# Block-sparse attention and a gated projection on one core: eleven more matmuls of ones by ones in the first three steps

## The chip, the core and the metric

The kernel runs on one core of one Trainium2 chip. A core has five engines that run their own instruction streams and wait for one another by semaphores: TensorE (PE in the rows; its weight loads are PEld), VectorE (DVE), ScalarE (ACT), GpSimd (POOL) and SyncE (SP), which here only issues transfers. TensorE reads SBUF and writes PSUM. The metric is the device time of one execution in microseconds; the median of the runs of the kernel before is 371.38 us.

## The reference, cut to what matters

Four batches, 8 heads, 768 positions in 24 blocks of 32, head size 64. The mask lets a block of queries see its neighbours, the first and the last block and three drawn blocks; the first and last blocks see everything.

```python
scores = scale * np.matmul(q, k.transpose(0, 1, 3, 2))
scores = np.where(mask, scores, -1000000000.0)
scores = scores - np.max(scores, axis=-1, keepdims=True)
attn = np.exp(scores)
attn = attn / (np.sum(attn, axis=-1, keepdims=True) + 1e-09)
out = np.matmul(attn, v)
# then, with x = the heads side by side (B, S, 512):
gate = 1.0 / (1.0 + np.exp(-gate_pre))   # gate_pre: a causal convolution of 5 taps over x
val = x @ w_val
result = gate * val @ w_out
```

## The kernel before, in words

The work is cut into units. A unit is a pair of neighbouring query blocks of one batch (11 pairs in a batch), or one of the two end blocks, for all 8 heads. The loop at line 762 runs over steps n, one unit entering per step. In a step the program issues, in this order for TensorE: the scores of unit n (`scores`, lines 409 to 466: 16 small f32 matmuls, which the trace shows as 32 passes, into two PSUM tiles `sc`, one for each half h of the heads), the product with the values of unit n-2 (`values`, line 479: `av<-va` and `av<-vb`), the transposition of a finished pair (`xp`), and the transposes of the weights of unit n-1 (`transposes`, line 468: `pt`), with matmuls of the projection (`vp`, `op`) put between them later on. Every engine executes its instructions in the order of the program; the class `InOrder` (line 77) ties each to the one before.

Between TensorE's pieces lie the other engines' parts: VectorE takes the row maxima of the scores (`mx`, line 457), ScalarE makes the exponentials from them (`pe`, line 462, two activations for each half h) and copies the transposes out of PSUM (`ptr`, line 475). GpSimd and ScalarE copy the key blocks of a pair together (`kg`, lines 326 to 348), ScalarE scales the queries (`qc`), and GpSimd gathers the value rows (`vb`).

The score tiles come from a pool of three buffers (line 71), two for each unit. So the second tile of unit 1 takes the buffer that the first half of unit 0 had, and the second tile of unit 2 the one that the first half of unit 1 had. Each must wait until ScalarE has read that half. Since the matmuls of the two halves alternate, everything behind them on TensorE waits with them.

At the very start there is nothing to multiply until queries and keys have arrived. There the program multiplies a tile of ones by itself 17 times into a PSUM tile `idle` that nothing reads (lines 110 to 114):

```python
    idle = ps_moe.tile([128, 512], F32, tag="mo", name="idle")
    for _ in range(WARM):
        matmul(idle[:, 0:256], ones[:, 0:128], ones, start=True, stop=True)
```

`idle` is one of two buffers of the tag "mo", which the transposition `xp` takes first in step 3.

Of the kernel before, what the change touches and what calls it, by code (L numbers as in the profile page):

```python
# [36 lines left out]
COPY_AHEAD = 2  # L37
WIDE, SPLIT = 2, 4
WARM = 17
HI_MOE = 2  # L40

COPIED = [{0: POOL, 1: POOL, 2: POOL, 3: ACT, 4: ACT, 5: ACT}, {0: POOL, 1: POOL, 2: ACT}, {}, {}]
# [22 lines left out]
def attention_moe(ctx, tc, qb, kb, v, ve, sampled, w_val, conv_w, w_out, ident_in, slot_in, out):  # L65
# [30 lines left out]
    matmul, transpose = pe.matmul, pe.transpose  # L96
# [13 lines left out]
    ones = const.tile([128, 256], F32, name="ones")  # L110
    pool.memset(ones, 1.0)
    idle = ps_moe.tile([128, 512], F32, tag="mo", name="idle")
    for _ in range(WARM):
        matmul(idle[:, 0:256], ones[:, 0:128], ones, start=True, stop=True)
    warm = const.tile([128, 1], F32, name="warm")
    dve.memset(warm, 0.0)
    act.activation(warm, warm, AF.Exp)
# [45 lines left out]
    def indices(b):  # L163

        row = const.tile([128, NB], F32, tag=f"row{b % 2}", name="row")
        dve.tensor_scalar_add(row, base, float(b * S - B * S))
        dve.tensor_tensor(out=row, in0=row, in1=valid, op=ALU.mult)
        dve.tensor_scalar_add(idx[:, b, :], row, float(B * S))
# [18 lines left out]
    def run(calls):  # L187
        while calls:
            calls.pop(0)()
# [106 lines left out]
    def block_numbers(pr, eng):  # L296

        mine = [n for n in range(2 * NR) if COPIED[pr.bt.b].get(n, SP) == eng]
        if not mine:
            return  # L300
        first = NR * PAIRS[pr.p][0] + mine[0]
        _, regs = nc.values_load_multi_w_load_instructions(
            sm[0:1, first : first + len(mine)], engines=[eng], min_val=0, max_val=NB - 1,
            skip_runtime_bounds_check_because="block numbers are drawn from [0, 24)",
        )
        for n, reg in zip(mine, regs):
            yield 5 + 4 * (n // NR) + n % NR, reg
# [101 lines left out]
    def scores(un):  # L409
        pr = un.pr  # L410
        un.P = []
        if pr.glob:
            lo = [ps_sc.tile([128, 512], F32, tag="sc", name="s0") for _ in range(2)]
            places = ((ps_moe, "mo"),) * 2 if pr.bt.b < HI_MOE else ((ps_sc, "sc"), (ps_pt, "pt"))
            hi = [space.tile([128, 512], F32, tag=tag, name="s1") for space, tag in places]
# [52 lines left out]
    def transposes(un):  # L468
        un.PT = []
        for p in un.P:  # L470
            pt = ps_pt.tile([128, 4, 128], F32, tag="pt", name="pt")
            for c in range(4):
                transpose(pt[:, c, :], p[:, 128 * c : 128 * c + 128], ident)
            t = three.tile([128, 4, 128], F32, tag="ptr", name="ptr")
            act.copy(t, pt)
            un.PT += [t[:, c, :] for c in range(4)]
            yield
# [43 lines left out]
    def finish(pr):  # L521
        if pr.p == 0:
            if pr.bt.b >= 2:

                while len(batches[pr.bt.b - 2].read) < 2 * len(TILES[pr.bt.b - 2]):
                    fill()
                    prepare(4)
            pr.bt.xT = two.tile([128, CH, KW - 1 + S], F32, tag="xT", name="xT")
            dve.memset(pr.bt.xT[:, :, 0 : KW - 1], 0.0)
        xT = pr.bt.xT  # L530
        near = units[max(step[0] - 1, 0) : step[0] + 1]
        spare = pr.bt.b < 2 and not may_project() and not any(un.pr.glob for un in near)
        space, tag = (ps_moe, "mo") if spare else (ps_sc, "sc")
        xp = space.tile([128, 4, 128], F32, tag=tag, name="xp")
        for j in range(2):
            transpose(xp[:, j, :], pr.x[:, j].rearrange("p h d -> p (h d)"), ident)
        yield
        o = KW - 1
        xv = xp[:, 0:2, :].rearrange("p j (c s) -> p c j s", c=CH)
        if pr.glob:  # L540
            for e, s0 in ((0, 0), (1, S - BLK)):
                act.copy(xT[:, :, o + s0 : o + s0 + BLK], xv[:, :, e, :])
        else:
            s0 = o + PAIRS[pr.p][0] * BLK
            act.copy(xT[:, :, s0 : s0 + 2 * BLK], xp[:, 0:2, :].rearrange("p a (b s) -> p (a b) s", b=2))
        pr.bt.done.add(pr.p)
        for t, (r0, rn) in enumerate(TILES[pr.bt.b]):
            need = {p for p in range(NP - 1) if any(r0 <= i * BLK < r0 + rn for i in PAIRS[p])}
            if r0 == 0 or r0 + rn == S:
                need.add(-1)  # L550
            if t not in pr.bt.queued and need <= pr.bt.done:
                pr.bt.queued.add(t)
                queue_rows(pr.bt, t)
# [128 lines left out]
    def store():  # L682
        while stores:
            sp.dma_start(*stores.pop(0))
# [27 lines left out]
    def may_project():  # L712
        return "all" in decoded and to_project and step[0] > max(to_project[0][0].ready)

    def fill(times=1):
        for _ in range(times):
            if may_project():
                run(late)
                advance(to_project)
# [21 lines left out]
    def freed(k):  # L741

        return units[min(k, N - 1)].pr.seq if k >= 0 else -1

    def more(which, upto, load):
        if at[which] < len(pairs) and pairs[at[which]].seq <= upto:
            load(pairs[at[which]])
            at[which] += 1
            return True

    def until(which, n, do):
        while at[which] < min(len(pairs), pairs.index(units[min(n, N - 1)].pr) + 1):
            do(pairs[at[which]])
            at[which] += 1
# [7 lines left out]
    for n in range(N + LAG_V):  # L762
        step[0] = n

        def more_keys():
            return more("keys", freed(n - 1) + RING, load_keys)

        def more_values():
            return more("values", freed(n - LAG_V - 1) + VRING, load_values)

        if n == 0:
            more_keys()
            numbers_first = {eng: list(block_numbers(pairs[0], eng)) for eng in (POOL, ACT)}
            until("scaled", 0, scale)
            indices(0)
            until("copied", 0, copy_keys)
            more_keys()
            until("copied", 1, copy_keys)
            more_values()
        else:  # L780
            while more_keys() or more_values():
                more_values()
        until("scaled", n + (SCALE_AHEAD if n else 1), scale)
        store()
        k = len(staged)
        if k < 2 * CH and n >= WEIGHTS_AT[k] and (k < 4 or k - 4 in decoded):
            next(weights)

        second_half = []
        if n < N:  # L790
            second_half.append(scores(units[n]))
            if not (n and units[n - LAG_T].pr.glob and units[n - LAG_T].pr.bt.b < HI_MOE):
                run(second_half)
        if n == 0:
            more_keys()
        until("copied", n + COPY_AHEAD, copy_keys)
        if n == 0:
            while more_keys() or more_values():
                more_values()
        if 0 <= n - LAG_V < N:  # L800
            values(units[n - LAG_V])
        if n >= LAG_V:
            while more("values", freed(n - LAG_V) + VRING, load_values):
                pass
        ending = [finish(units[n - LAG_X].pr)] if n >= LAG_X and units[n - LAG_X].last else []
        full = n < N and units[n].pr.glob and units[n].pr.bt.b >= HI_MOE
        for end in ending:
            if not full:
                next(end)

        def end_pairs():
            while ending:
                for _ in ending.pop(0):
                    pass

        if 0 <= n - LAG_T < N:
            pieces = 3 if units[n - LAG_T].pr.glob else 2
            for half, _ in enumerate(transposes(units[n - LAG_T])):
                at_half = 2 * n + min(half, 1)
                run(second_half)  # L820
                run(waiting)
                if half + 1 == pieces:
                    run(copies)
                    end_pairs()
                fill(int(FILLS[at_half]))
                holding[0] = half + 1 < pieces and not may_project()
                prepare(int(STEPS[at_half]))
                holding[0] = False
        else:
            fill(1)  # L830
            prepare(int(STEPS[2 * n]))
        if n == N + LAG_V - 1:
            ending.append(finish(units[N - 1].pr))
        end_pairs()
# [53 lines left out]
```

## Time and profile before

| what | value |
|---|---|
| three runs | 369.98, 371.38 and 376.13 us, median 371.38 us |
| the profiled execution | span 372.1 us; no other time of it is given |
| mean granted TensorE clock in it | 0.986 |
| busy: TensorE, VectorE, ScalarE, GpSimd | 94%, 73%, 68%, 39% of the span |
| TensorE in the chain that ended last | 78% of the span |

In a row of the timeline the first number is the start in us from the start of the span, the second the time from there to the end of the last instruction of the row. Instructions that follow one another and are alike share a row. The bracket tells how long the engine had been idle and what is thought to have ended that. The ends of matmuls are modelled, while a semaphore that another engine waits for is real: when VectorE starts a reduction, the scores are there. An f32 matmul has two passes, so a row of 34 passes stands for 17 matmuls. The rows of stretches give, for each stretch, its length, each engine's busy time, then the granted TensorE clock as a share of full speed, the share of the DMA engines and GB/s.

### The profile page before, as it was taken

Reading aid. Unit: us, or ns where it says so; the run is one execution under the profiler, and the core shown is the slowest. Engines: PE = TensorE matmul, PEld = TensorE weight load, DVE = VectorE, ACT = ScalarE, POOL = GpSimd, SP = SyncE. Lnnn points to the kernel's source line nnn. Section 1 sums busy time; section 2 is a strip of 40 time slices with the busy share of each in tenths; the row PEclk is TensorE's granted clock in tenths of the full one; section 3 lists DMA queues with packets and bytes.
Section 4 is the critical chain, followed back from the end, with each engine's and each line's share of the span. In section 5 each row is a group of like instructions: output and inputs, shape, how many; then the busy total and the mean of one; then the engine's idle time right before and its main releaser. Section 6 shows DMA issues by size and latency. Waiting matters only on the chain.

```text
span 372.1 us, 15481 instructions
## 1 busy us (share of the span) xinstructions
PE 349.9 (94%) x6274; PEld 276.1 (74%) x6274; DVE 270.6 (73%) x618; ACT 254.3 (68%) x619; POOL 144.9 (39%) x237
## 2 busy tenths in 40 slices
PE   8689998888998999999999999999999999999995
PEld 7456665556666787788779877787888779889894
DVE  4246789888978888678978867577669865979540
ACT  2568689899787857758687587666658766764421
POOL 1856683866573333633352063522531143000000
PEclk9959999999999999999999999999999999999999
DMA  7978886889987365798879367898664373110102
GB/s 229 278 241 277 283 281 226 237 219 299 286 257 248 109 167 146 188 315 232 262 203 289 107 173 214 218 288 250 192 195 130 98 232 99 55 58 28 75 11 85
DMA packets 52582, 72.35 MB, mean 194 GB/s; under 512 B 6944, under 2 KB 34720, under 8 KB 52512
## 3 DMA queue, kind: packets, MB, share of 16 engines
q1 hardware_dynamic: 44896, 47.69, 42.0%
q0 software_dynamic: 7040, 23.43, 22.1%
q8 instruction: 50, 0.82, 0.9%
q10 hardware_dynamic: 576, 0.24, 0.2%
q14 instruction: 20, 0.16, 0.2%
HBM read 65.05 MB, written 6.29 MB: 192 GB/s over the span
## 4 chain that ended last, share of the span: by engine, by line
PE 78%; DVE 8%; ACT 7%; issue 4%; another core or an unknown queue 1%; DMA 1%; ACTq 0%; DVEq 0%
PE vp L83 18%; PE op L83 18%; PE av L83 15%; PE pt L83 11%; PE sc L83 10%; PE xp L83 4%; PE s L83 3%; DVE mx L83 2%; ACT pe L83 2%; ACT ptr L83 2%; DMA sb<-in_sampled 1%; DVE xl L83 1%; DVE wst L83 1%; ACT first L83 1%
## 5 line engine op out<-in xcount | busy, mean ns | idle before, releaser
L83 POOL DMA_INDIRECT vb<-in_v,idx x88 | 87.4, 993 | 158.9 <-PE av L83 129.9
L83 ACT ACTIVATE pe<-sc,mx 128x256 f32<-128x256 f32 x176 | 69.6, 476 | 50.2 <-DVE mx L83 46.3
L83 DVE SCALAR_TENSOR_TENSOR th<-xT,cw,th 128x384 f32<-128x384 f32 x128 | 79.2, 626 | 7.5 <-ACT th L83 5.5
L83 DVE TENSOR_REDUCE mx<-sc 128x2 f32<-128x512 f32 x88 | 56.8, 684 | 38.1 <-PE sc L83 24.6
L83 ACT COPY ptr<-pt 128x512 f32<-128x512 f32 x112 | 64.4, 603 | 9.6 <-PE pt L83 7.1
L83 PE MATMUL sc<-kg,qc 64*32 64x256 f32 x1408 | 54.6, 388 | 6.9 <-DVE cst L83 3.4
L83 POOL COPY kg<-k 128x256 f32<-128x256 f32 (+1 forms) x143 | 56.8, 434 | 9.1 <-DMA k<-in_k 8.0
L83 PE MATMUL op<-wo,yh 128*128 128x512 f32 x192 | 53.6, 401 | 0.0
L83 PE MATMUL vp<-xh,wv 128*128 128x384 f32 x256 | 51.3, 341 | 0.0
L83 PE MATMUL pt<-ident,pe 128*128 128x128 f32 x352 | 50.9, 280 | 0.0
L83 PEld LDWEIGHTS av<-va,ptr 128*32 128x32 f32 (+1 forms) x1056 | 32.2, 119 | 24.9 <-issue 16.4
L83 PE MATMUL av<-va,ptr 128*32 128x65 f32 (+1 forms) x1056 | 42.7, 228 | 4.0 <-issue 3.1
L83 PEld LDWEIGHTS pt<-ident,pe 128*128 128x128 f32 x352 | 42.0, 144 | 3.3 <-DMA qc<-in_q 0.4
L83 PEld LDWEIGHTS vp<-xh,wv 128*128 128x128 f32 x256 | 44.2, 188 | 0.2
L83 PEld LDWEIGHTS sc<-kg,qc 64*32 64x32 f32 x1408 | 24.1, 107 | 26.9 <-issue 16.9
L83 PEld LDWEIGHTS op<-wo,yh 128*128 128x128 f32 x192 | 34.7, 188 | 6.6
L83 PE MATMUL av<-vb,ptr 128*32 128x65 f32 x1408 | 38.3, 224 | 1.3 <-issue 1.3
L83 PEld LDWEIGHTS av<-vb,ptr 128*32 128x32 f32 x1408 | 30.3, 111 | 3.3 <-issue 1.8
L83 PE MATMUL op<-wo,yl 128*128 128x512 f32 x96 | 31.6, 410 | 0.0
L83 ACT CAST yh<-y 128x384 fp32r<-128x384 f32 x32 | 16.6, 519 | 20.4 <-DVE y L83 19.8
L83 DVE SCALAR_TENSOR_TENSOR y<-th,vp 128x384 f32<-128x384 f32 x32 | 17.6, 549 | 13.7 <-PE vp L83 12.3
L83 PE MATMUL vp<-xl,wv 128*128 128x384 f32 x128 | 27.3, 335 | 0.0
(72 smaller groups left out, 441.1 us busy)
## 6 DMA issues: line engine op xcount, KB each, us to landing
kg<-in_k SPq DMA_DIRECT2D x165, 64.0 KB
vn<-in_v SPq DMA_DIRECT2D x12, 520.0 KB
qc<-in_q SPq DMA_DIRECT2D x48, 128.0 KB
k<-in_k SPq DMA_DIRECT2D x12, 512.0 KB
out<-ot SPq DMA_DIRECT2D x23, 256.0 KB
va<-in_v SPq DMA_DIRECT2D x44, 130.0 KB
wst<-in_w_val SPq DMA_DIRECT2D x4, 512.0 KB
wst<-in_w_out SPq DMA_DIRECT2D x4, 512.0 KB
```

Of the source, the lines that this page charges most:

```text
L83: made = getattr(self.eng, name)(*args, **kwargs)
```

## The change

The loop of the 17 matmuls becomes a function, and the steps n = 1 and n = 2 call it ahead of their scores, for 7 and for 4 more of the same matmul. They read and write what the first 17 did.

```diff
 WARM = 17
+MORE = {1: 7, 2: 4}
 HI_MOE = 2
...
-    for _ in range(WARM):
-        matmul(idle[:, 0:256], ones[:, 0:128], ones, start=True, stop=True)
+
+    def keep_busy(times):
+        for _ in range(times):
+            matmul(idle[:, 0:256], ones[:, 0:128], ones, start=True, stop=True)
+
+    keep_busy(WARM)
...
             next(weights)
 
+        keep_busy(MORE.get(n, 0))
         second_half = []
         if n < N:
             second_half.append(scores(units[n]))
```

On TensorE the first three steps read so before (kg_143 is the keys' buffer of unit 0, kg_144 of unit 1, kg_145 of unit 2; `pt` here are the transposes of unit 0):

```order
L83 MATMUL idle<-ones 128x256 x16
L83 MATMUL sc<-kg_143,qc 32x256 [waits Activation_49,Pool_49]
L83 MATMUL sc<-kg_143,qc 32x256 x15
L83 MATMUL sc<-kg_144,qc 32x256 [waits Activation_49,Pool_49]
L83 MATMUL sc<-kg_144,qc 32x256 [waits DVE_49,Activation_49]
L83 MATMUL sc<-kg_144,qc 32x256 x14
L83 MATMUL pt<-ident,pe 128x128 [waits DMAHW3_49]
L83 MATMUL sc<-kg_145,qc 32x256 [waits DVE_49,Activation_49,Pool_49]
L83 MATMUL sc<-kg_145,qc 32x256 [waits DVE_49,Activation_49]
L83 MATMUL sc<-kg_145,qc 32x256 x14
```

And so with the change:

```order
L84 MATMUL idle<-ones 128x256 x16
L84 MATMUL sc<-kg_143,qc 32x256 [waits Activation_49,Pool_49]
L84 MATMUL sc<-kg_143,qc 32x256 x15
L84 MATMUL idle<-ones 128x256 x7
L84 MATMUL sc<-kg_144,qc 32x256 [waits Activation_49,Pool_49]
L84 MATMUL sc<-kg_144,qc 32x256 [waits DVE_49,Activation_49]
L84 MATMUL sc<-kg_144,qc 32x256 x14
L84 MATMUL pt<-ident,pe 128x128 [waits DMAHW3_49]
L84 MATMUL idle<-ones 128x256 x4
L84 MATMUL sc<-kg_145,qc 32x256 [waits DVE_49,Activation_49,Pool_49]
L84 MATMUL sc<-kg_145,qc 32x256 [waits DVE_49,Activation_49]
```

The seven stand between the scores of unit 0 and those of unit 1, the four between the transposes of unit 0 and the scores of unit 2. None of the eleven waits for anything. The order and the waits of all other instructions of TensorE, and those of the other engines, stay as they were.

## Rows read from the trace of the kernel before

**Rows 1.** The page: span, and the granted clock in 40 slices.

```profile
span 372.1 us, 15481 instructions
...
PEclk9959999999999999999999999999999999999999
```

**Rows 2.** Stretches of the start: length, busy times, clock, DMA share, GB/s.

```profile
16.00:18.00 2.00, 1.40 (x32) 0.86 (x33) 0.46 (x3) 2.00 (x8) 1.53 (x3) 0.89 0.90 286
...
20.00:22.00 2.00, 0.59 (x2) 0.00 (x0) 0.82 (x2) 0.81 (x2) 2.00 (x5) 0.50 0.77 270
...
26.00:28.00 2.00, 2.00 (x24) 1.70 (x16) 1.19 (x5) 1.71 (x5) 1.62 (x6) 0.55 0.63 170
28.00:32.00 4.00, 3.55 (x89) 2.60 (x88) 1.47 (x4) 2.44 (x9) 3.38 (x8) 1.00 0.97 337
```

**Rows 3.** TensorE's timeline, 11 to 34 us: start, length, instructions, idle time before.

```profile
11.70 1.48 PE L83 MATMUL sc<-kg,qc 64*32 64x256 f32 x34
16.60 1.10 PE L83 MATMUL sc<-kg,qc 64*32 64x256 f32 x30 [3.42 <-DVE cst L83]
17.63 1.97 PE L83 MATMUL pt<-ident,pe 128*128 128x128 f32 x8
19.53 1.06 PE L83 MATMUL sc<-kg,qc 64*32 64x256 f32 x2
22.08 1.96 PE L83 MATMUL sc<-kg,qc 64*32 64x256 f32 x30 [1.50 <-ACT pe L83]
23.97 1.41 PE L83 MATMUL av<-va,ptr 128*64 128x65 f32 x16
25.30 1.09 PE L83 MATMUL av<-vb,ptr 128*32 128x65 f32 x32
26.33 1.79 PE L83 MATMUL pt<-ident,pe 128*128 128x128 f32 x8
28.05 1.09 PE L83 MATMUL sc<-kg,qc 64*32 64x256 f32 x32
...
30.61 0.67 PE L83 MATMUL av<-vb,ptr 128*32 128x65 f32 x32
31.21 0.44 PE L83 MATMUL xp<-ident,x 128*128 128x128 f32 x2
31.48 1.04 PE L83 MATMUL pt<-ident,pe 128*128 128x128 f32 x8
32.45 1.09 PE L83 MATMUL sc<-kg,qc 64*32 64x256 f32 x32
```

**Rows 4.** VectorE's timeline: the maxima of units 0, 1 (two rows) and 3.

```profile
14.98 1.29 DVE L83 TENSOR_REDUCE mx<-sc 128x2 f32<-128x512 f32 x2 [4.58 <-remote]
...
20.46 0.69 DVE L83 TENSOR_REDUCE mx<-sc 128x2 f32<-128x512 f32 x1 [4.00 <-PE pt L83]
21.87 0.69 DVE L83 TENSOR_REDUCE mx<-sc 128x2 f32<-128x512 f32 x1 [0.72 <-remote]
...
30.50 1.29 DVE L83 TENSOR_REDUCE mx<-sc 128x2 f32<-128x512 f32 x2 [2.78 <-PE sc L83]
```

**Rows 5.** ScalarE's timeline: exponentials of units 0 and 1, copies of unit 0.

```profile
15.71 1.57 ACT L83 ACTIVATE pe<-sc,mx 128x256 f32<-128x256 f32 x4 [3.48 <-DVE mx L83]
...
21.19 0.84 ACT L83 ACTIVATE pe<-sc,mx 128x256 f32<-128x256 f32 x2 [2.40 <-issue]
...
23.33 1.07 ACT L83 COPY ptr<-pt 128x512 f32<-128x512 f32 x2
```

**Rows 6.** TensorE's timeline: passes of the 17 matmuls, in two windows.

```profile
1.12 5.91 PE L83 MATMUL idle<-ones 128*128 128x256 f32 x13 [1.12 <-POOL ones L83]
...
8.15 3.62 PE L83 MATMUL idle<-ones 128*128 128x256 f32 x16
```

**Rows 7.** A long stretch later on, same columns as rows 2.

```profile
130.00:200.00 70.00, 69.80 (x1307) 55.82 (x1306) 55.74 (x128) 49.69 (x117) 30.39 (x40) 1.00 0.77 222
```

**Rows 8.** TensorE's timeline: a wait between two later units.

```profile
57.45 0.66 PE L83 MATMUL pt<-ident,rest 128*128 128x128 f32 x4 [1.17 <-ACT ptr L83]
```

## The prediction, made before the changed kernel had run

> **What bounds the kernel now.** [...] (1 - 0.89) x 2 + 4 x 1.0 + (1 - 0.55) x 2 = 5.1 us of clock are missing, which at half speed is a stretch of 10.2 us, from about 17.6 to 27.8 us.
>
> What TensorE did before the clock fell stands in its timeline [rows 3]: the scores of unit 0 from 11.70 us (32 of the 34 passes; the last two belong to unit 1), then 3.42 us of nothing, then from 16.60 the scores of unit 1. The name behind that idle time is a guess of the profile. By the program the second tile of unit 1 waits for ScalarE's exponentials of unit 0, and two of these four end at 15.71 + 0.84 = 16.55 us [rows 5]. They wait for the maxima at 14.98 [rows 4]. A second wait lies at 20.59 to 22.08 us, for the same kind of release: maxima of unit 1 at 20.46, exponentials at 21.19, scores of unit 2 at 22.08.
>
> Whether time gained at 28 us is still there at the end is read from the later stretches [rows 7]: between 130 and 200 us TensorE is busy for 69.80 of 70 us. It is the bound from there on, and whatever arrives there earlier ends earlier.
>
> **What the change costs.** One of the new matmuls has two passes. At full clock 16 passes take 3.62 us [rows 6], 0.23 each, so a matmul costs 0.45. The first 13 passes take 5.91 us [rows 6], 0.45 each and twice as much: 0.9 us a matmul at half clock. (The page shows 1.00 there, before the first change of clock on record.)
>
> The seven follow the scores of unit 0, from about 12.7 us (11.70 + 1.48 less two passes [rows 3]). 7 x 0.45 = 3.2 us, to about 15.9. Unit 1's scores can't start before 16.55 anyway, so they cost nothing, with 0.6 us to spare. The idle time ahead of them shrinks from 3.42 to about 0.7 us.
>
> The four follow the transposes of unit 0. These take 1.97 us at half clock, and 1.04 us where the clock is full [rows 3], so they end at about 18.7; 4 x 0.45 = 1.8 takes it to 20.5 us. The scores of unit 2 began at 22.08, and below I get 20.67 as the earliest they can. They cost nothing either, again only at full clock.
>
> One cost the trace doesn't show. The maxima of unit 0 start at 14.98 though the last recorded pass of its scores is over by 12.8 [rows 4, 3]. If only the signal is late, the seven run as above. If the scores themselves last until 14.96, the seven start there, end at 18.1 and hold unit 1's scores up by 1.5 us. So 0 to 1.5 us. I take 0: all 34 passes from 11.70 on, unit 1's two with them, are recorded within 1.48 us, so TensorE had gone on to the next unit by then.
>
> **What it brings.** With the clock kept, the steps from the scores of unit 2 run as the steps behind them do. From 22.08 to 28.05 us is 5.97 us for scores, values and transposes; the next such step takes 32.45 - 28.05 = 4.40 us, with an `xp` in it that the earlier step doesn't have [rows 3]. That is 1.6 us, or up to 2.0 with the `xp` (0.44) counted. By its parts: scores 1.96 to 1.09, values 0.67 for 1.09 in their second part, transposes 1.04 for 1.79; but the 0.9 of the scores is lost again, because the values wait for ScalarE's copies of unit 0, which begin at 23.33 [rows 5] and let them start at 23.97 [rows 3]. I take 1.6.
>
> Next, the scores of unit 2 may start earlier. From the start of unit 1's scores to its maxima there were 20.46 - 16.60 = 3.86 us, and for unit 3 at full clock 30.50 - 28.05 = 2.45 [rows 3, 4]. From maxima to the next scores 22.08 - 20.46 = 1.62. With 2.45 they start at 16.60 + 2.45 + 1.62 = 20.67, which is 1.4 us earlier. But unit 0, at full clock, needed 14.98 - 11.70 = 3.28, almost what unit 1 needed. So 0 to 1.4; from unit 0's 3.28 it would be 0.6. It is the nearest row in place and state, and I take 0.6.
>
> Sum: 0 + 0 - 1.6 - 0.6 = -2.2 us. Against the profiled execution's span of 372.1 that is 369.9. The median of the three runs is 0.7 lower, and I take the same off: **369.2 us**. With the ends of the terms the gain is 0.1 (1.6 less 1.5) to 3.4 us (2.0 + 1.4): 371.3 to 368.0.
>
> **Rivals.** *The clock falls anyway, and the four get in the way: slower.* Pauses remain: 0.7 us ahead of unit 1's scores, and between the four and unit 2's scores up to 1.7 us. Between them stand 1.04 us of transposes. If the clock falls at about 17.6 us as now, transposes end at 19.6 as before, and four matmuls at 0.9 end at 23.2, where the scores of unit 2 started at 22.08: 1.1 us later, 372.5 us on the scale of the median. It decides by whether the four last longer than 22.1 - 19.6 = 2.5 us. Against it: later pauses of 1.17 us [rows 8] leave the clock at full [rows 1], and each later step has transposes too. For it: TensorE did run transposes and scores from 17.6 to 20.6 us, and the clock didn't come back before 27.8 [rows 2, 3]. Chance 0.13.
>
> *All of the half clock comes back.* If every piece of TensorE work in that stretch were on the path, 5.1 us would return: 366.3 us. [...] Against it: in the stretch of 20 to 22 us TensorE is busy for 0.59 of 2 us [rows 2], and in both pauses it waits for ScalarE, whose clock is another. Chance 0.05.
>
> *The seven hold unit 1's scores up.* The bound above, 1.5 us, eats nearly all of the 1.6 us: 371.3 us. For it speaks how late the maxima of units 0 and 1 are; against it, that a late signal alone explains the same. Chance 0.15.
>
> *It does nothing that shows.* The fall may not come in every execution: the runs span 369.98 to 376.13, and one profile shows one of them. If the middle run had a shorter stretch at half clock than the profiled one, 371.4 us stays. Or VectorE and ScalarE, which work through 30 to 130 us beside TensorE, take the gain back. Chance 0.12.
>
> **How the numbers follow.** The forecast, clock kept and 1.6 to 3.4 us gained, has the remaining 0.55. The predicted time is its 369.2. Its own ends are 368.0 and 369.8; with the two cases that end at 371.3 and 371.4 that is 0.82 of the chance, and a median of a few runs can be off by about 1 us (the two lower runs differ by 1.4). So the range is 366.9 to 372.3 us, which leaves out the full return of the clock and most of the slower case. Within 2% means within 7.4 us, about what a measurement of this kernel can tell from no change. No case comes near that on either side, so same gets 0.96, and faster and slower 0.02 each for runs that scatter as far as the third one did (4.8 us above the median) on top of the outermost cases.
>
> **What would show it in the changed profile.** The clock line without its 5, and stretches of 1.00 from 16 to 28 us. Passes of ones at 0.23 us or less, the seven over before 16, the four before 21 us. Scores of unit 1 still at 16.6; if they start near 18, the seven held them up. Scores of unit 2 between 20.7 and 22.1, and 4.3 us or so from there to unit 3's. From 130 us on the same rows as before, earlier by about 2 us. The forecast is wrong if the clock still falls, if the scores of unit 2 start after 22.1, or if a wait for ScalarE or VectorE between 30 and 130 us has grown by what was gained.

## The result, and the profile after

| | before | after |
|---|---|---|
| median of 21 runs each, us | 371.38 (369.98 to 376.13) | 374.05 (371.28 to 379.95) |
| ratio of the two, 95% interval | | 1.0058 [1.0032, 1.0084] |
| profiled execution's span, us | 372.1 | 378.2 |

Forecast were 369.2 us and a range of 366.9 to 372.3. The kernel got slower, by 0.6%: outside the range and on the other side of zero, though well within 2%. The medians take in all runs, while a ratio leaves out those runs of a kernel that lie more than 1.5% above its fastest (on some chips of the experiments 12 to 19 of 29 runs of before, and few of after), so a ratio can lie well above that of the medians. The profiled execution of after is the longest of its runs (379.95 us); 4.5 us of its excess lie around one wait near 272 us that comes and goes in both kernels (experiments, fourth group), so the reading below stops ahead of it.

The page of after, the lines of [rows 1], and its stretches, those of [rows 2]:

```profile
span 378.2 us, 15525 instructions
...
PEclk9989999999999999999999999999989999999999
```

```profile
16.00:18.00 2.00, 1.57 (x34) 0.73 (x33) 0.57 (x3) 2.00 (x8) 1.53 (x3) 1.00 0.91 222
20.00:22.00 2.00, 1.13 (x5) 0.31 (x3) 0.09 (x1) 0.00 (x0) 1.97 (x5) 1.00 0.91 304
22.00:24.00 2.00, 0.48 (x16) 0.34 (x23) 1.46 (x4) 1.37 (x4) 0.41 (x2) 0.97 0.69 217
24.00:28.00 4.00, 4.00 (x77) 2.81 (x63) 1.84 (x5) 4.00 (x14) 1.63 (x6) 0.59 0.47 154
28.00:32.00 4.00, 3.33 (x87) 2.22 (x85) 1.44 (x5) 2.20 (x7) 3.42 (x8) 1.00 0.96 306
```

The stretches that [rows 2] leaves out, of before:

```profile
18.00:20.00 2.00, 2.00 (x10) 1.37 (x8) 0.00 (x0) 0.79 (x3) 1.39 (x3) 0.50 0.95 337
22.00:24.00 2.00, 1.92 (x32) 0.70 (x32) 0.83 (x3) 1.43 (x5) 0.33 (x2) 0.50 0.72 206
24.00:26.00 2.00, 2.00 (x49) 1.69 (x48) 1.29 (x2) 2.00 (x9) 0.51 (x2) 0.50 0.67 239
```

So before had a granted clock of 0.50 in all four stretches from 18 to 26 us, 10.2 us at half speed with the parts on either side. After, the full clock holds through 16 to 18 and 20 to 22 us, where it was 0.89 and 0.50. It still falls, but late: 2 x 0.03 + 4 x 0.41 = 1.7 us of clock are missing, 3.4 us at half speed in place of 10.2. The clock was kept for longer, and the time didn't follow. TensorE's timeline of after, as in [rows 3], shows where it went:

```profile
11.44 1.09 PE L84 MATMUL sc<-kg,qc 64*32 64x256 f32 x32
12.47 3.29 PE L84 MATMUL idle<-ones 128*128 128x256 f32 x14
15.69 0.62 PE L84 MATMUL sc<-kg,qc 64*32 64x256 f32 x2
16.74 1.09 PE L84 MATMUL sc<-kg,qc 64*32 64x256 f32 x30 [0.43 <-issue]
17.76 1.09 PE L84 MATMUL pt<-ident,pe 128*128 128x128 f32 x8
18.69 1.89 PE L84 MATMUL idle<-ones 128*128 128x256 f32 x8
20.51 0.62 PE L84 MATMUL sc<-kg,qc 64*32 64x256 f32 x2
23.52 1.70 PE L84 MATMUL sc<-kg,qc 64*32 64x256 f32 x30 [2.40 <-DVE words L84]
...
28.27 1.09 PE L84 MATMUL sc<-kg,qc 64*32 64x256 f32 x32
...
32.94 1.09 PE L84 MATMUL sc<-kg,qc 64*32 64x256 f32 x32
```

The scores of unit 1 start at 16.74 (before 16.60), those of unit 2 at 23.52 (before 22.08), of unit 3 at 28.27 (28.05), and of unit 4 at 32.94 (32.45). So what the clock gives back between 16 and 28 us is spent ahead of unit 2's scores, in a wait of 2.40 us (before 1.50). Its end is in VectorE's timeline, the maxima of units 0 and 1 as in [rows 4], in ScalarE's, the exponentials of unit 1, the first two of which the scores of unit 2 wait for, and in GpSimd's, whose DMA_INDIRECT rows are the gathers of value rows (the last fence is GpSimd's of before):

```profile
15.12 1.29 DVE L84 TENSOR_REDUCE mx<-sc 128x2 f32<-128x512 f32 x2 [4.84 <-remote]
21.91 1.29 DVE L84 TENSOR_REDUCE mx<-sc 128x2 f32<-128x512 f32 x2 [5.34 <-remote]
```

```profile
22.63 1.57 ACT L84 ACTIVATE pe<-sc,mx 128x256 f32<-128x256 f32 x4 [3.71 <-DVE mx L84]
```

```profile
13.70 0.95 POOL L84 DMA_INDIRECT vb<-in_v,idx  x1 [0.30 <-issue]
...
20.02 0.95 POOL L84 DMA_INDIRECT vb<-in_v,idx  x1 [0.30 <-issue]
20.98 1.44 POOL L84 COPY kg<-k 128x256 f32<-128x256 f32 x5
```

```profile
18.70 0.95 POOL L83 DMA_INDIRECT vb<-in_v,idx  x1 [0.30 <-issue]
19.95 0.94 POOL L83 DMA_INDIRECT vb<-in_v,idx  x1 [0.30 <-issue]
```

Unit 1's scores are over at 16.74 + 1.09 = 17.83 us, a little later than the 17.70 of before. Its maxima wait 4.1 us more, to 21.91, which is 0.94 us after the last gather of a burst of four ends (20.97). Unit 0's start at 15.12, 0.47 us after the end of its gather (14.65). Before, with nearly the same gathers, one half of unit 1's maxima came at 20.46 and the other at 21.87: the first 0.81 us after the third gather of that burst (18.70 + 0.95 = 19.65), the second 0.98 after the fourth (20.89). After has both behind the fourth. That one release more is the loss here: before, two exponentials were over soon enough for unit 2's scores at 22.08. Why the first half's signal came out one gather earlier before, these two traces don't tell, and no run of the experiments shows it.

A second loss lies near 60 us. TensorE's timeline there, before (behind the row of [rows 8]) and then after:

```profile
58.04 1.23 PE L83 MATMUL sc<-kg,qc 64*32 64x256 f32 x28
59.71 0.62 PE L83 MATMUL sc<-kg,qc 64*32 64x256 f32 x4 [0.44 <-issue]
60.26 1.57 PE L83 MATMUL av<-vn,ptr 128*32 128x65 f32 x96
```

```profile
58.15 0.66 PE L84 MATMUL pt<-ident,rest 128*128 128x128 f32 x4 [1.18 <-ACT ptr L84]
58.74 0.78 PE L84 MATMUL sc<-kg,qc 64*32 64x256 f32 x6
60.87 1.07 PE L84 MATMUL sc<-kg,qc 64*32 64x256 f32 x26 [1.35 <-issue]
61.87 1.34 PE L84 MATMUL av<-vn,ptr 128*32 128x65 f32 x80
```

No other engine is named behind this stop ("issue"). It comes after the same count of passes in both, the 850th, and in both it ends some 1.3 us after a transfer of 0.02 MB of instructions has landed (before 58.39 and 59.71, after 59.56 and 60.87). All 19 traces of this case have a stop there, each with one such transfer that landed 1.3 to 1.5 us before its end. The 11 new matmuls are 22 passes, so the 850th is now the 6th pass of these scores and not the 28th. That TensorE waits there for these instructions is inferred from their landing; if it does, 22 passes less lie between the wait for ScalarE and the stop to cover the transfer. The shift of after against before goes from 0.70 us (57.45 to 58.15) to 1.61 (60.26 to 61.87), and is 1.75 at pass 4000 (224.60 to 226.35 us, the ones not counted).

So this trace of after, against this one of before, has 0.70 us from the first 57 us and 0.9 from the stop. How far that holds for other executions, the table below shows.

### The profile page after: what moved, and what is told of

Same layout as the page of the kernel before. It is cut to its first block, busy times and chain, and to the rows that moved or that the text cites. A ratio compares the mean times of both kernels' runs of the same rounds, so it can differ in the third digit from the quotient of the medians.

```text
span 378.2 us, 15525 instructions
## 1 busy us (share of the span) xinstructions
PE 354.6 (94%) x6296; PEld 278.9 (74%) x6296; DVE 269.5 (71%) x618; ACT 254.0 (67%) x619; POOL 144.6 (38%) x237
## 4 chain that ended last, share of the span: by engine, by line
PE 70%; DVE 9%; ACT 7%; issue 5%; another core or an unknown queue 3%; SPq 3%; DMA 2%; ACTq 0%; DVEq 0%
PE vp L84 16%; PE op L84 15%; PE av L84 14%; PE pt L84 9%; PE sc L84 9%; PE xp L84 3%; DVE mx L84 3%; PE s L84 3%; ACT ptr L84 2%; SPq L84 2%; ACT pe L84 2%; DMA out<-ot 1%; DMA sb<-in_sampled 1%; DVE words L84 1%
## 5 line engine op out<-in xcount | busy, mean ns | idle before, releaser
L84 DVE TENSOR_REDUCE mx<-sc 128x2 f32<-128x512 f32 x88 | 56.6, 684 | 39.4 <-PE sc L84 22.5
L84 PE MATMUL pt<-ident,pe 128*128 128x128 f32 x352 | 49.7, 274 | 0.1
L84 PEld LDWEIGHTS pt<-ident,pe 128*128 128x128 f32 x352 | 40.6, 140 | 3.7 <-issue 0.6
L84 DVE SCALAR_TENSOR_TENSOR y<-th,vp 128x384 f32<-128x384 f32 x32 | 17.6, 549 | 13.4 <-PE vp L84 12.2
```

What stands on the lines that cost most here:

```text
L84: made = getattr(self.eng, name)(*args, **kwargs)
```

## Experiments

**Theory.** On the chip of these traces GpSimd's gathers hold TensorE's signals back until one of them is over, so the length of that stretch is GpSimd's, the clock in it is worth little, and the instructions added move a stop for code. **Rivals:** the seven or the four hold up the scores behind them; the number of new instructions alone is the cost; the difference is no larger than what two loads of one kernel differ by.

All medians and ratios stand against runs of the kernel before on the same chip. The times of passes are starts on TensorE in the profiled execution, the ones not counted; the half clock is worked out from stretches of 2 to 5 us up to 36 us; the stop is the idle time ahead of the next pass after 850, the ones counted. "Held": where gathers run, maxima start 0.4 to 1.1 us after the end of one, up to 4.1 us behind the last score pass. "Prompt": the maxima of units 0 to 3 start within 0.15 us of it, gathers or not. All traces of one chip are of one kind.

| run | chip | median, beside before | ratio | half clock, us | pass 790 | stop, us | pass 820 | pass 4000 |
|---|---|---|---|---|---|---|---|---|
| before | held |  |  | 10.2 | 58.20 | 0.44 | 60.26 | 224.60 |
| after | held | 374.05, 371.38 | 1.0058 | 3.4 | 58.90 | 1.35 | 61.87 | 226.35 |
| e1 the seven alone | prompt | 371.84, 369.60 | 1.0123 | 3.4 | 54.25 | 0.74 | 57.17 | 219.99 |
| e2 the four alone | prompt | 369.29, 369.60 | 1.0081 | 0 | 52.32 | 0.46 | 54.40 | 216.24 |
| e3 wide ones | prompt | 367.98, 369.60 | 1.0001 | 3.4 | 53.96 | 0.25 | 55.30 | 221.80 |
| e4 tiny matmuls | prompt | 370.27, 369.60 | 0.9983 | 3.4 | 52.43 | 0.60 | 55.42 | 218.29 |
| e5 after | prompt | 370.08, 368.96 | 1.0120 | 0 | 51.81 | 0.60 | 54.03 | 216.58 |
| e6 before | prompt | 372.33, 368.96 |  | 3.4 | 53.16 | 1.43 | 56.21 | 220.06 |
| e7 before, no gathers | prompt | 373.64, 368.96 |  | 3.4 | 52.48 | 0.15 | 54.25 | 217.68 |
| e8 after, no gathers | prompt | 369.69, 368.96 |  | 0 | 50.65 | 0.66 | 52.94 | 215.59 |
| e9 after | prompt | 371.74, 369.01 | 1.0165 | 0 | 51.23 | 0.80 | 53.65 | 216.21 |
| e10 wide ones | prompt | 370.98, 369.01 | 1.0044 | 0 | 52.11 | 1.12 | 54.32 | 223.37 |
| e11 wide ones, three | prompt | 370.21, 369.01 | 1.0032 | 0 | 52.64 | 1.30 | 53.66 | 221.24 |
| e12 before | prompt | 371.90, 369.01 | 1.0069 | 0 | 53.32 | 0.61 | 55.55 | 217.28 |
| e13 after | held | 375.92, 372.05 | 1.0088 | 0 | 56.02 | 1.08 | 58.72 | 222.59 |
| e14 before | held | 373.63, 372.05 | 0.9991 | 0 | 55.46 | 0.55 | 57.63 | 221.60 |
| e15 after, early stores | held | 383.22, 372.05 | 1.0201 | 0 | 55.49 | 0.98 | 58.09 | 227.93 |
| e16 before, early stores | held | 384.32, 372.05 | 1.0330 | 3.4 | 56.05 | 0.71 | 58.39 | 229.01 |
| e17 before, no gathers | held | 370.32, 373.88 | | 3.4 | 53.95 | 0.80 | 56.37 | 221.07 |

Read down the columns, two executions of one kernel differ: before has 220.06 and 217.28 us at pass 4000 on two prompt chips, 224.60 and 221.60 on two held ones. In the six pairs of traces that differ by the ones alone, the stop is longer with them in five (0.44 and 1.35, 0.55 and 1.08, 0.71 and 0.98, 0.61 and 0.80, 0.15 and 0.66), and shorter in the sixth (1.43 and 0.60).

### First group: parts of the change

e1 keeps `MORE = {1: 7}` alone, e2 `MORE = {2: 4}` alone. e3 does the same ones in matmuls of 512 columns, 15 instead of 28 with the warm-up; e4 is the kernel before with 11 tiny matmuls behind the warm-up, so that the number of instructions is that of after and the time isn't.

```diff
 e3: -            matmul(idle[:, 0:256], ones[:, 0:128], ones, start=True, stop=True)
     +            matmul(idle[:, 0:512], ones[:, 0:128], ones[:, 0:512], start=True, stop=True)
 e4: +    for _ in range(11):
     +        matmul(idle[0:32, 0:8], ones[:, 0:32], ones[:, 0:8], start=True, stop=True)
```

> Only the seven matmuls of ones ahead of unit 1's scores, none ahead of unit 2's. Signal theory (the signal that unit 1's scores are done comes out late, at 21.9 us instead of 20.4, because TensorE goes on with the four matmuls behind them): unit 1's maxima start near 20.4 us as in the kernel before, unit 2's scores near 22.1, time like before or a little less. If it is the seven that delay it, unit 1's maxima start near 21.9 and unit 2's scores near 23.5. Code theory (each matmul of ones adds 4 instructions of TensorE, and the place where its code must be fetched near 60 us moves): 28 instructions more, so about two thirds of the 0.9 us that the whole change lost near 60 us.

> Only the four matmuls of ones ahead of unit 2's scores. The clock falls near 17.6 us as in the kernel before, so the four run at half clock, 0.9 us each. Signal theory: unit 1's maxima start near 21.9 us and unit 2's scores at 23.3 or later, time 1 to 2 us above before. If the seven are the cause: maxima near 20.4 us, unit 2's scores at about 23.2 because the four themselves last until then. Code theory: 16 instructions more, a third of the 0.9 us near 60 us.

> The change with matmuls of ones twice as wide (512 columns), so half as many for the same time: 15 in all against 28, 8 instructions fewer than the kernel before has. Signal theory alone: unit 2's scores near 23.5 us, all of the loss of the change stays (ratio about 1.006). Code theory: TensorE's wait in the scores near 60 us is back at 0.4 us or below, and about 0.9 us of the loss is gone (ratio about 1.002).

> The kernel before with eleven very small matmuls of ones (8 columns, 32 wide) behind the 17: as many more instructions as the change has (44), but almost no time and no TensorE work in the two waits. Code theory: the wait in the scores near 60 us grows from 0.4 to about 1.3 us, time 0.9 us above before (ratio about 1.0025). Signal theory alone: unit 2's scores near 22.1 us and no difference to the kernel before.

The intervals are [1.0059, 1.0188], [1.0025, 1.0137], [0.9948, 1.0055] and [0.9909, 1.0056]. Eleven more matmuls alone show no cost, though the interval of e4 reaches 1.0056, about the loss in question. Either part alone gives a ratio above 1, which the fourth run of the third group makes worth less; by its median e2 is even below before. The code theory's figures for the stop came out in part: 0.25 us in e3 for 0.4 or below, but 1.12 in the same kernel as e10, and 0.60 in e4 for 1.3. The profiles brought something not expected: on this chip the maxima of units 0 to 3 start within 0.11 us of the last score pass, with the same gathers running. So e1 and e2 can't tell which of the two blocks of ones makes the held signal of the first chip later.

### Second group: the same two kernels again, and without the first gathers

e5 is after and e6 before, unchanged. e7 and e8 are before and after with the gathers of the first three pairs replaced by plain loads of fixed rows (the values there differ):

```diff
+            if b == 0 and pr.p < 3:
+                sp.dma_start(pr.vb[:, j, :], v[128 * pr.p : 128 * pr.p + 128, :])
+                continue
```

> The changed kernel once more, to have it beside the kernel before on a chip other than the first if so it falls. Code theory: TensorE stops at the 850th of its passes, as in every kernel so far, for longer than the kernel before does; ratio above 1. If matmul signals come out at once here (0.05 us behind the last pass of the scores), unit 2's scores start near 19.2 us and the part of the loss that came from the late signal on the first chip is absent: ratio 1.000 to 1.004. If they come late as on the first chip: ratio about 1.006.

> The kernel before itself, for its trace on the same chip as the others of this call. Code theory: TensorE stops at its 850th pass, and at the 345th if its code is late there. Signal theory: if the signal of the scores is late, it is late whenever a gather of GpSimd runs while the scores end, and out within 0.1 us otherwise.

> The kernel before with the six gathers of the first three pairs replaced by plain loads of fixed rows on SyncE's queue (their values are those of other rows). Signal theory with gathers as the cause: the maxima of units 0 and 1 start within 0.2 us of the last pass of their scores, so unit 0's near 13.4 instead of 15.0 and unit 2's scores 4 us or more earlier than 22.1. If the scores themselves last that long, or the full transfer queues delay the signal, the maxima stay near 15.0 and 20.4.

> The same in the changed kernel. Signal theory: unit 0's maxima start within 0.2 us of its last pass, unit 1's scores directly behind the seven matmuls of ones (about 15.9 us), which now hold them up by 1 us or more, and unit 1's maxima within 0.2 us of their last pass. If gathers aren't the cause: unit 1's maxima near 21.9 as in the change.

e5 has a ratio of 1.0120 [1.0042, 1.0198], above the 1.000 to 1.004 expected for signals that come out at once; the others are one execution each. TensorE's timeline of e5, then of e6:

```profile
12.65 3.29 PE L84 MATMUL idle<-ones 128*128 128x256 f32 x14
15.87 1.09 PE L84 MATMUL sc<-kg,qc 64*32 64x256 f32 x32
...
19.65 1.09 PE L84 MATMUL sc<-kg,qc 64*32 64x256 f32 x32
...
23.29 1.09 PE L84 MATMUL sc<-kg,qc 64*32 64x256 f32 x31
```

```profile
14.42 1.09 PE L83 MATMUL sc<-kg,qc 64*32 64x256 f32 x30 [0.78 <-ACT pe L83]
...
16.74 1.74 PE L83 MATMUL sc<-kg,qc 64*32 64x256 f32 x32 [0.20 <-POOL kg L83]
...
21.57 0.66 PE L83 MATMUL av<-vb,ptr 128*32 128x65 f32 x30 [1.69 <-DMA vb<-in_v,idx]
...
23.32 1.10 PE L83 MATMUL sc<-kg,qc 64*32 64x256 f32 x16
```

With prompt signals the seven do hold up unit 1's scores, by 15.87 - 14.42 = 1.45 us, and with the four unit 2's come 2.9 us later. At unit 3's scores both are level again (23.29 and 23.32): the kernel without ones waits there for gathered rows until 21.57. In this pair the gathers set the end of the stretch too, by their data. In e12 and e9, on another prompt chip, unit 3's scores are level as well (22.55 and 22.62), but there the kernel without the ones waits last for GpSimd's copy of the keys.

In e7 and e8 the maxima were prompt as well, but so they were in e5 and e6 on that chip. They show nothing on the held signals.

### Third group: what a ratio is worth

e9 is after, e12 before beside itself; e10 is e3 again, and e11 is wide with `MORE = {1: 3}`.

> The changed kernel, timed beside its wide form and the kernel before on one chip. If signals come out at once here: the seven last until 15.8 us and hold unit 1's scores up by about 1.4 us, the four hold unit 2's up by about 3 us, most of it in front of the wait for unit 0's gathered values (about 21.5 us) that was there before. Code theory: stops at passes 345 and 850, ratio 1.003 to 1.010. Theory that it is only the hold-up: ratio as that of the wide form.

> The wide form again (15 matmuls of ones against 28 in the change, 17 before, the same time on TensorE as in the change). Code theory: faster than the change of the same call by 0.5% or more, like the kernel before (ratio 0.996 to 1.003). If the hold-up of the scores is what costs: as slow as the change.

> The wide form with 3 matmuls' worth of ones ahead of unit 1's scores (1.3 us) and none ahead of unit 2's: 11 matmuls of ones in all. Where signals come at once the three end before unit 1's scores can start (14.4 us) and hold nothing up. Hold-up theory: faster than the wide form with 7 and 4 by up to 1 us. Code theory alone: like that one. Both: the best of the four, ratio 0.990 to 1.000. The clock may fall once for 3.4 us in the wait for unit 0's gathered values, as in the kernel before.

> The kernel before against itself: ratio 1.000; how far it is from that shows what a ratio of this size is worth here. Every theory: the same.

e9 came to 1.0165 [1.0106, 1.0223], e10 to 1.0044 [0.9993, 1.0095] (medians 370.98 and 369.01), e11 to 1.0032 [0.9973, 1.0092] (370.21). The kernel before beside itself gave 1.0069 [1.0003, 1.0136] and 371.90 against 369.01. A ratio of 0.7% with an interval that leaves out 1 can come from no change at all, so nothing under 1% of the first group decides anything, and neither version that was meant to be better is shown to be. The median of after (371.74) is about that of before beside itself (371.90) on this chip, so 1.0165 decides no more.

### Fourth group: equally many runs, and the wait near 260 us

e13 is after and e14 before, with equally many runs on one chip. In e5 to e9 and e12 TensorE waits for 2.2 to 5.0 us ahead of a late projection. In after the two rows are, from TensorE's timeline and from the list of waits:

```profile
275.16 1.85 PE L84 MATMUL vp<-xh,wv 128*128 128x384 f32 x8 [2.69 <-ACT ot L84]
```

```profile
ACT ot L84 <- DMA out<-ot: 4.2, 1, 4.2
```

ScalarE can't write the output tile because the store of two tiles ago has not landed. e15 (after) and e16 (before) issue the stores from ScalarE at once:

```diff
-            stores.append((out[m.bt.b, m.t + r * 128 : m.t + r * 128 + 128, :], ot))
+            act.dma_start(out[m.bt.b, m.t + r * 128 : m.t + r * 128 + 128, :], ot)
```

> The changed kernel once more, on another chip, with as many rounds as e14. Theory A (the extra matmuls move the early work by -1 to -2 us up to pass 4000, and the rest is a wait near 260 us whose length is not tied to the change): its median lies within 2 us of e14's, on either side, and the profile has a wait of 0 to 5 us ahead of pass 4840. Theory B (the change itself costs 2 to 3 us): median 2 to 3 us above e14's, and its pass 4000 not earlier than e14's.

> The kernel before beside itself. Theory A: a ratio of up to 0.7% from 1 on either side can come again, with nothing changed; pass 4000 comes 1 to 2 us later than in e13. Theory B: ratio 1.000 within 0.3%, so that the 1.0069 of the earlier null run was a stray.

> The changed kernel with all but the last store issued by ScalarE right behind the copy into the output tile, instead of later by SyncE behind the key loads. Theory A: the wait of ScalarE for the store near 260 us goes (0 to 0.5 us), spread narrower, median 366 to 368 and 1 to 2 us below e16. Theory B: the wait goes too, but the median stays 2 us above e16. Rival: the stores issued earlier take the DMA engines from key and value loads, and the wait turns up there, median unchanged.

> The kernel before with the same early stores, without the extra matmuls. Theory A: 367 to 369, wait near 260 us gone; 1 to 2 us above e15. Theory B: 366, below e15 by 2. Rival: no change against the kernel before.

After against before here: 375.92 and 373.63, ratios to the same runs 1.0088 [1.0048, 1.0128] and 0.9991 [0.9944, 1.0039]. The intervals don't meet; on this chip the changed kernel is slower, by about 1%. Theory A of these expectations, a tie, did not hold. B's figures did: 2.3 us between the medians, a ratio of e14 within 0.3% of 1, and pass 4000 not earlier but 1.0 us later.

This chip holds signals as the first one did. e14 had the full clock through all stretches without any ones added. Its TensorE and VectorE:

```profile
17.45 1.09 PE L83 MATMUL sc<-kg,qc 64*32 64x256 f32 x30 [0.17 <-ACT pe L83]
...
21.79 0.22 PE L83 MATMUL av<-vb,ptr 128*32 128x65 f32 x1 [0.19 <-issue]
22.51 0.67 PE L83 MATMUL av<-vb,ptr 128*32 128x65 f32 x27 [0.50 <-issue]
```

```profile
22.61 1.29 DVE L83 TENSOR_REDUCE mx<-sc 128x2 f32<-128x512 f32 x2 [5.19 <-remote]
```

And e13's:

```profile
19.61 1.14 PE L84 MATMUL sc<-kg,qc 64*32 64x256 f32 x24
21.12 0.39 PE L84 MATMUL sc<-kg,qc 64*32 64x256 f32 x1 [0.37 <-issue]
22.55 0.69 PE L84 MATMUL sc<-kg,qc 64*32 64x256 f32 x7 [1.04 <-issue]
```

```profile
23.26 1.29 DVE L84 TENSOR_REDUCE mx<-sc 128x2 f32<-128x512 f32 x2 [4.12 <-PE sc L84]
```

Both have the last gather of the burst end at 21.5 us, and in both TensorE goes on at 22.5. In e14 unit 2's scores had been over since 18.54 and only their signal was late. In e13 the ones had pushed these scores to 19.61, so TensorE was stopped in the middle of them, with 7 passes left, and the maxima came 0.65 us later (23.26 to 22.61). The hold by the gathers is that of the first pair of traces, but the ones lose by it in another way: there a signal came out one gather later, here passes that were late were stopped. And one signal does not fit "until a gather is over": the maxima of unit 1 in e13 start at 17.41, 0.49 us behind their last pass, while a gather runs (16.79 to 17.76), and in e15 they do the same. Ahead of that, unit 0's signal was prompt in both kernels (12.71 and 12.76), so the seven held unit 1's scores up on this held chip, by 15.83 - 14.32 = 1.51 us. The stop at pass 850 grew here too, from 0.55 to 1.08 us.

e15 and e16 got slower, to 383.22 and 384.32 us (ratios 1.0201 [1.0121, 1.0282] and 1.0330 [1.0276, 1.0384]). The rival named with them had the wait turn up elsewhere, which holds, and the median unchanged, which doesn't. In e16 TensorE's timeline has

```profile
190.23 1.12 PE L83 MATMUL pt<-ident,pe 128*128 128x128 f32 x4 [5.26 <-ACT rest L83]
```

and behind it ScalarE, 7.8 us behind a value load (`ACT xh <- DMA va<-in_v`). That the stores kept this load waiting is argued, not shown. Since neither before, e13 nor e14 has the wait near 260 us, this pair can't tell what it does to the change. Its start repeats e13 and e14: in e15 TensorE stops inside unit 2's scores (0.41 and 0.85 us), and the maxima come 1.63 us after the last gather's end, in e16 1.07 us. Behind the release e16 then has 3.4 us of half clock, from 22.93 us on, and e15 none, which makes up for it: at unit 3's scores e15 is 0.66 us ahead (25.00 and 25.66), about as much as its gathers were (21.17 and 21.88).

### Last run: do gathers hold the signals?

e17 is e7 once more. Its later pairs still gather, and show which kind of chip it is.

> The kernel before with the first three pairs' gathers replaced by plain loads of fixed rows (their values differ). Only telling if the later pairs' gathers (29 to 45 us) show signals 1 us or more late on its chip. Theory (gathers hold TensorE's signals on such a chip): then the maxima between 12 and 26 us start 0.05 to 0.1 us after the last score pass, and unit 2's are over by 20 us. Rival (something else on such a chip, the first code fetches or loads): they are 1 to 6 us late as in e14, though no gather runs there. If the later signals come within 0.1 us, the chip is of the prompt kind and the run tells nothing.

It ran on a chip that holds signals. VectorE's timeline of e17, and GpSimd's first gathers:

```profile
12.76 1.29 DVE L83 TENSOR_REDUCE mx<-sc 128x2 f32<-128x512 f32 x2 [1.91 <-PE sc L83]
15.55 1.29 DVE L83 TENSOR_REDUCE mx<-sc 128x2 f32<-128x512 f32 x2 [0.78 <-PE sc L83]
18.51 1.29 DVE L83 TENSOR_REDUCE mx<-sc 128x2 f32<-128x512 f32 x2 [1.38 <-PE sc L83]
...
30.38 1.29 DVE L83 TENSOR_REDUCE mx<-sc 128x2 f32<-128x512 f32 x2 [0.54 <-PE sc L83]
```

```profile
22.32 1.13 POOL L83 DMA_INDIRECT vb<-in_v,idx  x1 [0.17 <-issue]
...
28.81 1.12 POOL L83 DMA_INDIRECT vb<-in_v,idx  x1 [0.30 <-issue]
```

The score passes ahead of these maxima end at 12.69, 15.47, 18.44 and 29.39 us. The first three maxima, with no gather running, start 0.07 to 0.08 us later; those of the last row (unit 4), with one running until 29.93, 0.99 us later. Taking the gathers away takes the delay away, on a chip that has it; GpSimd's key copies, which ran until 15.45, held nothing back. The theory is shown in this point, in one execution. By what means a gather holds a signal, no run tells. (The times, 370.32 us and 373.88 for before, are one execution each.)

## Why the prediction was wrong, step by step

- **The clock** would be kept from 16 to 28 us: half right. 10.2 us at half speed became 3.4; a wait of 2.40 us was left, and the fall came behind it (0.59 in 24 to 28 us). And the fall of the profile before wasn't the rule: of seven other traces without these ones (e4, e6, e7, e12, e14, e16, e17) five had 3.4 us and two none. The rival that the fall doesn't come in every execution had 0.12; its premise held, its 371.4 us didn't. The rival that had the kernel slower (0.13) went by a fall at 17.6 us, which didn't come.
- **The seven cost nothing**: right on the first chip (16.74 for 16.60), where unit 0's late signal covers them; 1.45 us on a prompt one and 1.51 in e13, where that signal came early too. That is near the 1.5 us of the prediction's bound and of the rival that had 0.15, but not by their reason: the scores of unit 0 did not last longer, those of unit 1 could have started at 14.42 and 14.32.
- **The four cost nothing**: on the first chip they were in nobody's way, since unit 2's scores began behind them, at 20.51, and then waited until 23.52. On a prompt chip unit 2's scores came 2.9 us later with them.
- **Unit 2's scores start earlier, by 0.6**: this step failed. They started 1.44 us later. The prediction took the 3.28 to 3.86 us from scores to maxima for TensorE's and VectorE's own time. It named "only the signal is late" as a possibility and didn't ask what the signal waited for. It was a gather of GpSimd, here the burst's last, which ended at 20.97 whatever TensorE's clock did (20.89 before).
- **The 1.6 us of unit 2's step at full clock**: the step from unit 2's to unit 3's scores did shorten, from 5.97 to 28.27 - 23.52 = 4.75 us, so 1.2 for 1.6. The prediction's own parts, 0.42 for the values and 0.75 for the transposes, make 1.2 as well; that they meet the measured step is luck, as 3.4 us of it ran at half clock. It only gave back most of the 1.44 just lost. From unit 3 to unit 4 came 0.27 more, which I did not trace to one cause.
- **What the prediction had no term for**: the 22 added passes move the stop at pass 850 from 28 passes behind a wait to 6 behind it, 0.44 to 1.35 us in this pair. The 850 was in the trace, as an "issue" row, and wasn't read. That the change makes it longer is likely, by five pairs of six, but its length scatters as much without the change (0.44 to 1.43 us in before, e6, e12 and e14).
- **All 5.1 us come back**: refuted. By that rival's count, 5.1 us for 10.2 at half clock, the 6.8 us less should have given 3.4 us; unit 3's scores came 0.2 later (28.27 for 28.05). TensorE's time in that stretch was not what the next scores waited for. ScalarE's own time didn't follow that clock: in before the first exponential at 15.71 us, with the clock full, took 474 ns, and the one at 21.19, with the clock at 0.50, 474 ns as well.
- **The starting point**: the sum takes the profiled span, 372.1 us, for a time 0.7 above the median. In the runs a time is 1.7 to 1.8 us longer than its span (379.95 for 378.2), so that execution lay about 2.5 us above the median. The 369.2 doesn't suffer, being the median less 2.2.

**What stays open.** In the two pairs of traces from chips that hold signals after is 1.0 and 1.75 us behind at pass 4000, of a difference of 2.2 (0.0058 x 371.4 us) and 2.3 us (375.92 - 373.63); two traces of before on such chips differ by 3.0 there, so these shifts are read in single executions and are not shown to be the 0.6% of the medians. On the prompt chips the changed kernel was 1.1 to 3.5 us ahead at pass 4000 (216.21 and 217.28, 216.58 and 220.06), and its medians still weren't lower than those of before (370.08 and 371.74 against about 369). The wait near 260 us eats such a lead in e5 and e9 (3.2 and 4.2 us), but it is 2.2 to 5.0 us in e6, e7 and e12 without the change, so I can't say that the change makes it longer. That after is slower stands on its first 21 runs and on e13 beside e14. Its medians lie 0.3 to 1.0% above those of before on all four chips, but before beside itself lay 0.8 and 0.4% above too (e12, e14). What would make it slower on prompt chips is open. Why some chips hold the signals and others don't, no run tells. None of these versions is shown to beat the kernel before.

## What to carry to other kernels

Before a stall is filled to keep TensorE's clock (five of the six traces with these eleven matmuls had no half clock up to 36 us, two of the eight without them), find what releases the first work behind it: where that is another engine's burst, here GpSimd's gathers, TensorE's clock in front of it was worth nothing (6.8 us less at half clock, and unit 3's scores 0.2 us later), and filler in the queue made TensorE late for the release (maxima 0.65 us later in e13 than in e14). Read the "issue" stops of TensorE by pass number; filler moved the one at pass 850 to other work, and it went from 0.44 to 1.35 us in the first pair. And run the kernel beside itself before believing a ratio under 1%.

## What the runs showed of the hardware

- While GpSimd gathers run, on some chips TensorE's signals reach VectorE late, 0.4 to 1.1 us after a gather's end, up to 4.1 us behind the last pass, and TensorE itself stops (0.37 and 1.04 us in e13); not every signal, for unit 1's in e13 came 0.49 us behind its last pass with a gather running. On the others VectorE started within 0.15 us of the last pass with the same gathers.
- TensorE stops at pass 850 in all 19 traces, whatever the passes do, for 0.15 (e7) to 1.43 us (e6), and goes on 1.3 to 1.5 us after an instruction transfer has landed; that it waits for its own code is inferred from this. The transfer is 0.02 MB in the profile.
- Two loads of the same kernel differed by 0.7% on one chip (e12), and by -0.1% on another (e14).
